# A fused transformer block on one core: the prologue's dense products as couples of 64-row halves

## The chip, the core and the metric

The kernel runs on one core of a Trainium2 chip. A core has a matrix engine (TensorE, PE in the profile; its weight loads are listed apart, as PEld), a vector engine (VectorE, DVE), an engine for activation functions (ScalarE, ACT), a general engine (GpSimd, POOL), and a queue engine (SyncE, SP) that here issues nearly all transfers between the device memory (HBM) and the on-chip memories. TensorE writes into PSUM, which has 128 partitions and eight banks of 512 float32 columns per partition; GpSimd doesn't touch PSUM in this kernel, so a result reaches it by way of a copy of ScalarE.

The metric is the device time of one execution in microseconds.

## The reference

The block takes one sequence of 2048 rows of 512 numbers. Cut to what matters:

```python
mod = (silu(c) @ w_mod).reshape(1, 6, 1, 512)
sa, ca, ga, sb, cb, gb = (mod[:, i] for i in range(6))
h = layernorm(x) * (1 + ca) + sa
q, k, v = split(h @ wqkv)                  # 32 heads of 16
p = softmax(einsum("bhqd,bhkd->bhqk", q, k) * 16 ** -0.5)
x = x + ga * (merge(einsum("bhqk,bhkd->bhqd", p, v)) @ wo)
h = layernorm(x) * (1 + cb) + sb
u = h @ w1 + b1                            # 512 -> 1792
x = x + gb * ((u * tanh(softplus(u))) @ w2)
```

All of it is float32. With 32 heads of only 16 numbers each, the scores of 2048 x 2048 per head are the bulk of the work.

## The kernel before, in words

**Precision.** A dense product is made of three products of rounded operands (type fp32r): high by high, high by low, low by high, where high is the rounded operand and low the rest. `mm3` queues these matmuls; for a contraction of 512 they are 12 of up to 512 columns, 128 rows deep. [...] 

**The attention.** Work goes in steps `t`, 16 of them to an item of four heads and 512 queries (`step`, L1316). Each step has two half steps, numbered `h` (2t and 2t+1), and everything that isn't on the main path is hung onto a half step with `at(h, f)` and issued by `run_hooks(h)`. The engines' instruction streams and the SP queue are in the order of these calls; an instruction that waits holds up all behind it on its engine.

The softmax needs the maximum of each row of scores before the exponentials. So items go through a first pass (`max_tile`, L561, or `max_pair`, L575: scores in the layout queries by keys, and a maximum of VectorE over them) and, 20 steps later (`PRO`), a second one (`score`, L614: scores in the layout keys by queries with the negative maximum as extra rows, and the exponential of ScalarE; `pv`, L628: the product with the values). A maximum of a whole item is turned by `neg_max` and `max_rows` (a transpose through PSUM, a copy on ScalarE, a product on VectorE, four small transfers into the queries' tile, L607).

**The stages.** First (0 to 47 us) comes the layer norm of x, its transposes, and the first slices of the key, query and value products (L325 to L543). Then comes the *prologue*, the steps t = -20 to -1, which this change is about: it has only the first pass, and beside it dense units. Then comes the *main stage* from t = 0, in which both passes and a dense unit run beside each other as 64-row halves, and last the tail (from some 1580 us).

**The prologue's step** (L1321 to L1336). Two calls of `max_pair`: each makes two matmuls with 64 rows (two heads of 16 numbers with extra rows, side by side on the two halves of the array) into a pair of neighbouring banks, and one reduction of VectorE over 128 x 1024. Then the hooks, then `whole_units(h, 7.2)`, which issues dense matmuls, all 128 rows deep, worth 7.2 matmuls of 512 columns. The pairs of banks come from a ring of six banks (`ring`, L151), so three pairs; the dense units use the banks "ms" and "acc" in turn.

**The dense units of the prologue.** `plan` (L1426) lists them: the values' first half for blocks 4 to 15 of 128 rows (12 units of 12 matmuls of 256 columns; two units are as long as one other unit), then the query slice 1 for the first 512 rows, the four units of key slice 1, and the first of key slice 2. Each unit's end is a `fin`. For the values (L285) it is a ScalarE copy into a store buffer, and after each fourth a transfer to HBM. For queries and keys (L250) it is a ScalarE copy `qf`, the rounding `qh` and the rest `ql` on GpSimd, and transfers two half steps later. `qh` and `ql` have two buffers, `qf` has one. The weights of a slice are loaded by `slice_load` (L226), rounded on ScalarE and their rest made on GpSimd by `slice_split` (L233); when that happens is in `planned` (L1431) with the exceptions `LATE_SPLIT` and `LATE_LOAD`.

**What else hangs on the prologue's half steps.** Early preparation of six weight tiles of the second dense layer (`early_prep`, L1483: load, rounding and rest on GpSimd, two stores each), the loads of the head pairs 2 and 3 at -22 and -2 (L1538, `load_pair`), of the values of the first item at -3 (L1528, `load_v`), and the four transfers of the maxima of item 0 at -6.

Of the kernel before, what the change touches and what calls it, by code (L numbers as in the profile page):

```python
# [8 lines left out]
F32 = mybir.dt.float32  # L9
# [9 lines left out]
def adaln_block(ctx: ExitStack, tc: tile.TileContext, x, wqkv, wo, w1, b1, w2, c, w_mod, out):  # L19
    nc = tc.nc  # L20
# [22 lines left out]
    CREDIT = 7.2  # L43
    LATE_SPLIT = {3: -8, 4: 4}
    LATE_LOAD = {3: -15, 4: -4, 5: 9}
# [101 lines left out]
    ring_at = [0]  # L147

    kept = []

    def ring(w=1):  # L151
        if w == 2 and ring_at[0] % 2:
            ring_at[0] += 1
        if kept and ring_at[0] % NRING == NRING - 1:
            ring_at[0] += 1
        b = ring_at[0] % NRING
        ring_at[0] += w
        return ring_t[:, b, :] if w == 1 else ring_t[:, b:b + 2, :]

    def bank(tag="ms"):  # L160
        return ring() if tag == "ring" else ps.tile([P, TB], F32, tag=tag, name="bk", bufs=1)

    def free_banks():
# [3 lines left out]
        for i in nc.cur_bb.bb.instructions:  # L167
# [55 lines left out]
    slices = {}  # L223
    put_away = set()
# [17 lines left out]
    def qk_unit(kind, ct, tb, tag):  # L242
# [7 lines left out]
        def fin(h=None):  # L250
            qh = qp.tile([P, TB], F32R, tag="qh", name="qh", bufs=2)
            ql = qp.tile([P, TB], F32R, tag="ql", name="ql", bufs=2)
# [3 lines left out]
            else:  # L256
                qf = pw.tile([P, TB], F32, tag="raw", name="qf", bufs=1)
# [317 lines left out]
    def max_pair(n, jq, kb):  # L575
# [9 lines left out]
        nc.vector.tensor_reduce(out=mxs[n][:, :, jq, kb:kb + 1], in_=pm, op=ALU.max, axis=AX.X)  # L585

# [722 lines left out]

    def maxima(n, u, s, others):  # L1310
# [5 lines left out]
    def step(t):  # L1316
# [4 lines left out]
        if t < 0:  # L1321
# [104 lines left out]
    plan = [(-PRO, 2, 0, range(4, 16)), (-PRO, 0, 1, (0,)), (-PRO, 1, 1, range(NB)), (-PRO, 1, 2, range(NB)),  # L1426
# [4 lines left out]
    def planned(i, a, tag):  # L1431
# [96 lines left out]
    at(-3, lambda: load_v(0))  # L1528
# [9 lines left out]
    for pp, h in ((2, -22), (3, -2)):  # L1538
        at(h, lambda pp=pp: load_pair(pp))
# [3 lines left out]

    for t in range(-PRO, T + 2):
        step(t)
        prep_step(t)
# [33 lines left out]
```

## Time and profile before

| | us |
|---|---|
| median of three runs | 1688.64 |
| lowest and highest of them | 1687.62, 1691.29 |
| profiled execution, its time | 1688.32 |
| its span | 1686.5 |
| PE busy in the span | 1670.4 (99%) |
| DVE busy | 1432.9 (85%) |
| ACT busy | 1357.4 (80%) |
| POOL busy | 812.5 (48%) |

The profile has one row per group of instructions. A row of the timeline gives the start, the length, the engine, the line of the kernel, the operation, what it writes and reads, the shapes and the number of instructions taken together, and in brackets the idle time of the engine before it with what ended that. A row of the chain of waits gives only start, length, engine and line: it is the path on which the end depends. `SPq` rows are transfers being issued by the SP queue, not their landing. In the rows of windows, the columns are the stretch, its length, then busy time and number of instructions of PE, PEld, DVE, ACT and POOL, then the granted clock of TensorE (1.00 is all of it), the busy share of the DMA engines, and GB/s.

### The profile page before, as it was taken

Reading aid. Unit: us, or ns where it says so; the run is one execution under the profiler, and the core shown is the slowest. Engines: PE = TensorE matmul, PEld = TensorE weight load, DVE = VectorE, ACT = ScalarE, POOL = GpSimd, SP = SyncE. Lnnn points to the kernel's source line nnn. Section 1 sums busy time; section 2 is a strip of 40 time slices with the busy share of each in tenths; the row PEclk is TensorE's granted clock in tenths of the full one; section 3 lists DMA queues with packets and bytes.
Section 4 is the critical chain, followed back from the end, with each engine's and each line's share of the span. In section 5 each row is a group of like instructions: output and inputs, shape, how many; then the busy total and the mean of one; then the engine's idle time right before and its main releaser. Section 6 shows DMA issues by size and latency. Waiting matters only on the chain.

```text
span 1686.5 us, 33920 instructions
## 1 busy us (share of the span) xinstructions
PE 1670.4 (99%) x12491; PEld 924.4 (55%) x12491; DVE 1432.9 (85%) x2372; ACT 1357.4 (80%) x2612; POOL 812.5 (48%) x839
## 2 busy tenths in 40 slices
PE   8999999999999999999999999999999999999998
PEld 6755655555445455555555455555555455555687
DVE  6998888888999988888889888888889888883377
ACT  7257777777778988888878998888878988889674
POOL 5555224655313664556323565556323664555442
PEclk9999999999999999999999999999999999999999
DMA  8877656777755334434355434534344433534261
GB/s 261 264 251 188 157 145 197 205 228 218 225 136 161 97 93 104 120 81 130 82 137 161 106 77 98 139 80 122 100 133 120 130 93 81 149 97 135 76 227 63
DMA packets 114983, 239.00 MB, mean 142 GB/s; under 512 B 24500, under 2 KB 50120, under 8 KB 108864
## 3 DMA queue, kind: packets, MB, share of 16 engines
q1 hardware_dynamic: 114808, 236.82, 49.7%
q8 instruction: 99, 1.62, 0.4%
q14 instruction: 68, 0.56, 0.1%
q10 hardware_dynamic: 8, 0.00, 0.0%
HBM read 180.48 MB, written 51.45 MB: 138 GB/s over the span
## 4 chain that ended last, share of the span: by engine, by line
PE 92%; DVE 3%; ACT 2%; DMA 1%; issue 1%; POOL 0%; SPq 0%; ACTq 0%; DVEq 0%; POOLq 0%
PE bk L636 29%; PE ring L618 22%; PE ring L569 19%; PE bk L134 11%; PE bk L127 3%; PE ring L127 2%; PE ring L1249 2%; DVE mx L571 2%; ACT pr L621 1%; PE ring L583 1%; DMA qa<-mt 0%; PE ring L952 0%; PE ring L598 0%; DMA xt<-in_A_x 0%; PE ring L134 0%
## 5 line engine op out<-in xcount | busy, mean ns | idle before, releaser
L571 DVE TENSOR_REDUCE mx<-ring 128x1 f32<-128x512 f32 x1968 | 1221.9, 681 | 150.9 <-PE ring L569 136.2
L621 ACT ACTIVATE pr<-ring 128x512 f32<-128x512 f32 x2048 | 1078.7, 603 | 207.8 <-PE bk L134 116.3
L569 PE MATMUL ring<-ka,qa 64*128 64x512 f32 x1968 | 818.3, 429 | 1.3 <-ACT pr L621 1.0
L618 PE MATMUL ring<-qa,ka 64*128 64x512 f32 x2048 | 759.0, 402 | 3.2 <-ACT pr L621 2.0
L636 PE MATMUL bk<-pr,vg 128*32 128x512 f32 x4096 | 545.1, 604 | 0.0
L569 PEld LDWEIGHTS ring<-ka,qa 64*128 64x128 f32 x1968 | 350.6, 184 | 326.4 <-DVE mx L571 251.4
L618 PEld LDWEIGHTS ring<-qa,ka 64*128 64x128 f32 x2048 | 373.6, 184 | 192.2 <-DVE mx L571 113.3
L134 PE MATMUL bk<-h,w 64*128 64x512 f32 (+1 forms) x1080 | 277.8, 390 | 0.0
L134 PE MATMUL bk<-w,a_h 64*128 64x512 f32 x632 | 210.8, 413 | 0.0
L134 PEld LDWEIGHTS bk<-h,w 64*128 64x128 f32 x1080 | 178.5, 184 | 9.2 <-ACT pr L621 1.5
L636 PEld LDWEIGHTS bk<-pr,vg 128*32 128x32 f32 x4096 | 81.2, 108 | 135.8 <-issue 126.5
L134 PE MATMUL bk<-w,a_l 64*128 64x512 f32 x316 | 124.0, 392 | 0.0
L134 PEld LDWEIGHTS bk<-w,a_h 64*128 64x128 f32 x632 | 106.7, 184 | 3.4 <-ACT hb L830 0.8
L1008 POOL TENSOR_TENSOR y<-yd,y 128x512 f32<-128x512 f32 x44 | 56.8, 1292 | 88.9 <-ACT yd L1007 79.5
L842 POOL TENSOR_SCALAR qq<-ee 128x512 f32<-128x512 f32 x25 | 15.5, 620 | 169.3 <-ACT ee L836 169.3
L858 POOL TENSOR_TENSOR qq<-qq,rr 128x512 f32<-128x512 f32 x42 | 54.1, 1289 | 85.8 <-ACT rr L852 85.8
L844 POOL TENSOR_TENSOR hb<-hb,ee 128x512 f32<-128x512 f32 x42 | 54.1, 1288 | 79.6 <-DVE ee L840 77.6
L134 PE MATMUL bk<-w,o_hl 64*128 64x512 f32 x288 | 79.3, 405 | 0.0
L96 POOL TENSOR_TENSOR a_l<-hb,a_h 128x512 fp32r<-128x512 f32 x53 | 73.1, 1379 | 4.4
L134 PEld LDWEIGHTS bk<-w,a_l 64*128 64x128 f32 x316 | 58.3, 184 | 2.8
L93 POOL TENSOR_SCALAR qh<-qf 128x512 fp32r<-128x512 f32 x27 | 16.7, 620 | 88.3 <-ACT qf L258 68.1
L134 PE MATMUL bk<-h_h,wl 64*128 64x512 f32 x168 | 57.3, 421 | 0.2 <-ACT pr L621 0.2
(222 smaller groups left out, 1901.3 us busy)
## 6 DMA issues: line engine op xcount, KB each, us to landing
ka<-kscr SPq DMA_DIRECT2D x124, 384.0 KB
w<-w2scr SPq DMA_DIRECT2D x56, 512.0 KB
w<-w1scr SPq DMA_DIRECT2D x46, 512.0 KB
vg<-vscr SPq DMA_DIRECT2D x32, 552.0 KB
qa<-qscr SPq DMA_DIRECT2D x124, 100.0 KB
kscr<-qh SPq DMA_DIRECT2D x16, 512.0 KB
qscr<-qh SPq DMA_DIRECT2D x32, 256.0 KB
w2scr<-hl SPq DMA_DIRECT2D x14, 512.0 KB
```

The costliest lines, as they stand in the source:

```text
L96: (nc.gpsimd if eng == "p" else nc.vector).tensor_sub(lo, src, hi.bitcast(F32))
L127: nc.tensor.matmul(acc, l, r, start=start, stop=stop)
L134: i = nc.tensor.matmul(acc, l[64 * g:64 * g + 64], r[64 * g:64 * g + 64], start=start and not then, stop=bool(stop and then))
L569: nc.tensor.matmul(pm, qt[64 * s:64 * s + 64, qs * P:(qs + 1) * P], kt[64 * s:64 * s + 64, kb * TB:(kb + 1) * TB], start=True, stop=True)
L571: nc.vector.tensor_reduce(out=mxs[n][:, s, 4 * j + qs, kb:kb + 1], in_=pm, op=ALU.max, axis=AX.X)
L618: nc.tensor.matmul(p_, kt[64 * s:64 * s + 64, kc * P:(kc + 1) * P], qt[64 * s:64 * s + 64, :], start=True, stop=True)
L621: e = nc.scalar.activation(pr, p_, AF.Exp, scale=SCALE)
L636: nc.tensor.matmul(accs[n][32 * h:32 * h + 32, :], vgs[n][:, o:o + 32], pts.pop((t, h)), start=(kc == 0), stop=(kc == 15))
L844: (nc.vector if tail else nc.gpsimd).tensor_mul(hb, hb, ee)
L858: nc.gpsimd.tensor_mul(qq, qq, rr)
L1008: nc.gpsimd.tensor_add(y[i], yd, y[i])
L1249: nc.tensor.matmul(po[i // 2][:, i % 2, :], l[:, s], w[:, r, :], start=(f == 0 and j == 0), stop=(f == FT - 1 and j == 2))
```

## The change

**Couples.** The prologue's dense matmuls are no longer issued with 128 rows. A generator (`lanes`) takes twelve slots at a time into one bank (a query or key unit, or two value units in the two halves of a bank); two such banks make a couple. A first turn over the couple issues, slot by slot, rows 0 to 63 of the one and rows 64 to 127 of the other, a second turn the remaining halves. Two couples are interleaved: first turn of one, first turn of the other, second turn of the one, second turn of the other. The second turn waits for a small ScalarE copy `seen`, which the next `max_pair` behind the first turn makes from its own scores. Each call of `max_pair` is followed by a call of `dense_slots` for three or four slots (3, 3, 3, 3, 4, 4, 4, 4, 4, 4 and again), where before two `max_pair` were followed by 7.2 slots at once. A couple's four or so ends (`fin`) come together, one half step after its second turn.

**Banks.** During the prologue the ring of `max_pair` has four banks, two pairs. The other two banks of the ring, "ms" and "acc" are the four beds of the two couples. After the last step the ring is six banks again.

**Order and buffers.** The query unit comes before the values. A slice is split directly in the `fin` that calls for it, where that is before half step -4, and key slice 2 is loaded at half step 7 behind that. Query and key units that end at half steps -4 to 2 take `qh` and `ql` from eight spare tiles (tiles that the attention's output uses later) and `qf` from the buffers of the exponentials.

**Loads.** Pair 3 is loaded at -10 (was -2), the first item's values at -7 (was -3).

**Dependencies.** The pass that declares instructions on different ring banks independent looks back over 96 instructions of the ring (was 32).

```diff
-    CREDIT = 7.2
-    LATE_SPLIT = {3: -8, 4: 4}
-    LATE_LOAD = {3: -15, 4: -4, 5: 9}
+    LATE_SPLIT = {4: 4}
+    LATE_LOAD = {4: -4, 5: 9}
...
-        b = ring_at[0] % NRING
+        b = ring_at[0] % ring_of[0]
...
-                for j, b, others, theirs in seen[-32:]:
+                for j, b, others, theirs in seen[-96:]:
...
+            late = h is not None and -4 <= h < 3
+            if late and not spares:
+                for v in range(2):
+                    both = ap.tile([P, DK, TB], F32R, tag=f"o_{v}", name="late", bufs=1)
+                    spares.extend(both[:, i, :] for i in range(DK))
+            if late:
+                qh, ql = spares.pop(), spares.pop()
...
+                qf = (ap.tile([P, TB], F32, tag=f"p{len(spares) // 2 % 2 * 2}", name="qf", bufs=3) if late else
+                      pw.tile([P, TB], F32, tag="raw", name="qf", bufs=1))
...
+        if waiting:
+            seen = ap.tile([P, 2], F32, tag="seen", name="seen", bufs=2)
+            e = nc.scalar.copy(seen, pm[:, :, 0])
+            for c in waiting:
+                c["after"] = e
+            waiting.clear()
...
+    COUPLES = 6
+    now, waiting = [0], []
+    beds = [ring_t[:, NRING - 2, :], ring_t[:, NRING - 1, :], "ms", "acc"]
+    def lanes():
+        def take():
+            bed = bank(beds[0])
+            beds.append(beds.pop(0))
+            slots, fins = [], []
+            while len(slots) < 12:
+                while not units or now[0] < units[0][0]():
+                    yield None
+                half = len(fins) * TB // 2
+                unit = units.pop(0)[1]
+                fins.append(unit(bed[:, half:]))
+                n = 2 if pe_queue[0][0].shape[-1] <= TB // 2 else 1
+                ms = [(*m[:3], m[3] and half == 0, m[4] and len(slots) * n + len(pe_queue) == 12 * n) for m in pe_queue]
+                slots += [ms[j:j + n] for j in range(0, len(ms), n)]
+                pe_queue.clear()
+            return slots, fins
+        def couple():
+            a = yield from take()
+            b = yield from take()
+            return {"two": (a, b)}
+        def turn(c, p):
+            (a, fa), (b, fb) = c["two"]
+            for j, both in enumerate(zip(a, b)):
+                for k in range(max(len(x) for x in both)):
+                    for x, g in zip(both, (p, 1 - p)):
+                        if k < len(x):
+                            mm_half(x[k], g, c["after"] if p and not j and not k else None, p)
+                yield len(a) - j - 1
+            if not p:
+                waiting.append(c)
+                return
+            for fin in fa + fb:
+                at(now[0] + 1, lambda fin=fin, h=now[0] + 1: fin(h))
+        for _ in range(COUPLES // 2):
+            c1 = yield from couple()
+            yield from turn(c1, 0)
+            c2 = yield from couple()
+            yield from turn(c2, 0)
+            yield from turn(c1, 1)
+            yield from turn(c2, 1)
+    def dense_slots(h, most):
+        now[0] = h
+        for _ in range(most):
+            if not next(lane, 0):
+                return
...
-            if second and tm % 16 == 15:
-                neg_max(tm // 16)
-            run_hooks(2 * t + 1)
+                if i and second and tm % 16 == 15:
+                    neg_max(tm // 16)
+                if not i:
+                    run_hooks(2 * t + 1)
+                dense_slots(2 * t + 1, 3 if (2 * tm + i) % 10 < 4 else 4)
...
-            whole_units(2 * t + 1, CREDIT)
+            if t == -1:
+                for _ in lane:
+                    pass
+                ring_of[0] = NRING
...
-    plan = [(-PRO, 2, 0, range(4, 16)), (-PRO, 0, 1, (0,)), (-PRO, 1, 1, range(NB)), (-PRO, 1, 2, range(NB)),
+    plan = [(-PRO, 0, 1, (0,)), (-PRO, 2, 0, range(4, 16)), (-PRO, 1, 1, range(NB)), (-PRO, 1, 2, range(NB)),
...
-                    at(split_at[i + 2], lambda: slice_split(*plan[i + 2][1:3], hi_eng="p" if h > 0 else "a"))
+                    split = lambda: slice_split(*plan[i + 2][1:3], hi_eng="p" if h > 0 else "a")
+                    split() if h < -4 else at(split_at[i + 2], split)
...
-    at(-3, lambda: load_v(0))
+    at(-7, lambda: load_v(0))
...
-    for pp, h in ((2, -22), (3, -2)):
+    for pp, h in ((2, -22), (3, -10)):
...
+    ring_of[0] = NRING - 2
     for t in range(-PRO, T + 2):
```

More of the change, by code (lines that the diff above doesn't have):

```diff
@@ L147, in adaln_block @@
     ring_at = [0]
+    ring_of = [NRING]
     kept = []
@@ L160, in bank @@
     def bank(tag="ms"):
+        if not isinstance(tag, str):
+            return tag
         return ring() if tag == "ring" else ps.tile([P, TB], F32, tag=tag, name="bk", bufs=1)
@@ L223, in adaln_block @@
     slices = {}
+    spares = []
     put_away = set()
@@ L250, in fin @@
         def fin(h=None):
-            qh = qp.tile([P, TB], F32R, tag="qh", name="qh", bufs=2)
-            ql = qp.tile([P, TB], F32R, tag="ql", name="ql", bufs=2)
+            late = h is not None and -4 <= h < 3
[5 more added lines that the diff above has]
+                qh, ql = spares.pop(), spares.pop()
+            else:
+                qh = qp.tile([P, TB], F32R, tag="qh", name="qh", bufs=2)
+                ql = qp.tile([P, TB], F32R, tag="ql", name="ql", bufs=2)
             if h is None:
@@ L256, in fin @@
             else:
-                qf = pw.tile([P, TB], F32, tag="raw", name="qf", bufs=1)
+                qf = (ap.tile([P, TB], F32, tag=f"p{len(spares) // 2 % 2 * 2}", name="qf", bufs=3) if late else
+                      pw.tile([P, TB], F32, tag="raw", name="qf", bufs=1))
                 nc.scalar.copy(qf, acc)
@@ L1308, in whole_units @@
                 cur["fin"] = None
+    COUPLES = 6
[41 more added lines that the diff above has]
+            yield from turn(c2, 1)
+    lane = lanes()
+    def dense_slots(h, most):
[3 more added lines that the diff above has]
+                return
     def maxima(n, u, s, others):
```

## The prediction

> **What bounds the kernel now.** I read the page's totals first, then windows over the first 130 us, since all that the change reorders runs there, then the chain of waits and the timeline from 45 to 110 us.
>
> ```profile
> PE 1670.4 (99%) x12491; PEld 924.4 (55%) x12491; DVE 1432.9 (85%) x2372; ACT 1357.4 (80%) x2612; POOL 812.5 (48%) x839
> ```
> ```profile
> 65.00:70.00 5.00, 5.00 (x38) 4.00 (x37) 4.53 (x5) 1.07 (x3) 4.83 (x6) 1.00 1.05 348
> 100.00:105.00 5.00, 4.38 (x31) 2.68 (x29) 5.00 (x10) 4.33 (x10) 1.89 (x2) 1.00 1.00 246
> ```
> ```profile
> 63.00 0.66 PE ring L583 x4
> 63.66 1.87 PE bk L127 x14
> ...
> 94.05 0.66 PE ring L583 x4
> 94.72 1.82 PE bk L127 x7
> ...
> 100.58 1.12 ACT pr L621 x2
> ...
> 102.48 0.23 PE bk L134
> ```
>
> PE is busy all the time, in the prologue too, but with DVE close behind (4.53 of 5 us) and the DMA engines full. In the chain a prologue step is 0.66 us for four score matmuls and 1.8 to 1.9 us for the dense ones. The row at 102 us is the main stage's rate: one pair of 64-row matmuls per 0.23 us. Four score matmuls would thus be 0.46, not 0.66.
>
> ```profile
> 65.46 0.74 PE L583 MATMUL ring<-ka,qa 64*128 64x512 f32 x4
> 66.00 2.36 DVE L585 TENSOR_REDUCE mx<-ring 128x2 f32<-128x1024 f32 x2 [0.15 <-PE ring L583]
> 66.12 0.54 PEld L127 LDWEIGHTS bk<-wl,h_h 128*128 128x128 f32 x4 [0.37 <-issue]
> ...
> 95.21 1.09 PE L127 MATMUL bk<-h_h,wh 128*128 128x512 f32 x4
> 96.14 0.40 PE L127 MATMUL bk<-h_h,wl 128*128 128x512 f32 x1
> ```
> ```profile
> L585 DVE TENSOR_REDUCE mx<-ring x40: 1212/1216/1227, 48.8 to 98.2; 128x2 f32<-128x1024 f32 x40
>   PE ring L583: 2.5, 9
> ```
>
> The weight loads pause 0.37 us, with no releaser, where the forms change from 64 to 128 rows; this is the lost time. A full matmul of 512 columns costs (1.09 - 0.40) / 3 = 0.23 us, the same as a pair of halves, so couples save nothing but the two changes of form in each step. Two reductions back to back take 2.36 us, one 1.216, so their pitch is 1.144 us; the 40 starts (48.8 to 98.2) are 1.267 us apart on average where 1.144 would do. DVE could be 0.12 us quicker in each half step.
>
> **The change part by part.**
>
> *Couples.* PE's work in the prologue is 40 score pairs and 144 slots, 184 x 0.235 = 43.2 us. VectorE's forty starts need 39 x 1.144 = 44.6 us and two small things more. So the bound passes from PE to DVE, and the gain is capped by it: if nothing else stood in the way, the last reduction would start at 48.83 + 44.6 + 0.67 = 94.1 instead of 98.2.
>
> *Two pairs of banks in place of three, at the start.* The ring's call count is 21 at the first `max_pair`. By six banks it gets 4 and 5; by four it gets 2 and 3, and bank 2 (20 modulo 6) holds the last key unit of the stage before.
>
> ```profile
> 48.09 0.62 ACT L89 CAST wh<-wr 128x512 fp32r<-128x512 f32 x1
> 48.23 0.69 DVE L96 TENSOR_TENSOR ql<-ring,qh 128x512 fp32r<-128x512 f32 x1 [1.25 <-ACT qh L89]
> 48.79 1.29 POOL L96 TENSOR_TENSOR wl<-wr,wh 128x512 fp32r<-128x512 f32 x1 [2.10 <-ACT wh L89]
> ```
>
> DVE reads that bank until 48.92, then PE's pair can go, and 0.54 us (65.46 to 66.00) later the first reduction: 49.55 in place of 48.83, 0.7 us lost. Behind it the query unit, now first, finds its weights (48.71 and 50.08) in time.
>
> *The maxima of item 0.*
>
> ```profile
> 88.85 0.34 DVE L592 TENSOR_REDUCE mm<-mx 128x16 f32<-128x64 f32 x2
> ...
> 89.26 0.28 PE L598 MATMUL ring<-ident,mm 128*32 128x128 f32 x1
> ...
> 91.38 0.33 DVE L601 SCALAR_TENSOR_TENSOR mt<-mh,lows,ring 32x128 fp32r<-32x128 f32 x1
> ...
> 91.77 2.79 SPq L607 DMA_DIRECT2D qa<-mt  x4
> ```
>
> The two DVE pieces stay, 0.67 us. The transpose takes a single bank of the four and makes the next pair skip one, onto banks that the last reduction still reads: that pair comes 0.54 us after it, less the 0.33 that DVE fills with L601, 0.2 us lost. Its form is another one, a pause of the 0.37 kind, of which I count 0.25. The half steps behind it all have four slots, 5 x 0.235 = 1.175 us on PE against 1.144: 0.03 for five of them. Together 0.6 us; the ends are 0.2 (the pair alone) and 1.0 (two full pauses besides).
>
> *Ends of units in bunches; slices split at once.* The query unit's end puts the rounding of key slice 1 onto ScalarE ahead of the copies that empty its two beds.
>
> ```profile
> 59.24 0.43 SPq L230 DMA_DIRECT2D wr<-in_A_wqkv  x1
> 59.78 1.54 SPq L1488 DMA_DIRECT2D ep<-in_B_w  x3
> ...
> 63.54 0.62 POOL L93 TENSOR_SCALAR ep<-ep 128x512 fp32r<-128x512 f32 x1 [8.22 <-DMA ep<-in_B_w]
> 65.09 0.37 ACT L287 COPY vq<-bk 128x256 f32<-128x256 f32 x1 [1.92 <-PE bk L127]
> ...
> 80.24 1.23 SPq L268 DMA_DIRECT2D qscr<-qh  x2
> 88.44 0.62 POOL L93 TENSOR_SCALAR qh<-qf 128x512 fp32r<-128x512 f32 x1 [3.32 <-DMA qscr<-qh]
> ...
> 95.49 0.59 ACT L258 COPY qf<-bk 128x512 f32<-128x512 f32 x1 [3.87 <-PE bk L127]
> 96.87 1.28 POOL L96 TENSOR_TENSOR ql<-qf,qh 128x512 fp32r<-128x512 f32 x1
> ```
>
> The load is issued at 59.24 whatever the prologue does, as what precedes it on SP is unchanged; a transfer issued 0.5 us later took 3.8 us, so it lands at about 63.0. Then 0.62 + 0.59 + 2 x 0.37 = 1.95 us of ScalarE: beds free at 65.0. The third couple asks for them at half step 14 of the prologue's 40, 49.55 + 13 x 1.144 + 0.3 = 64.7. PE waits 0.3. DVE has 1.144 - 0.54, some half a microsecond, in hand, but four-slot half steps follow that don't win it back: 0.2 us lost. With the longest landing seen (80.24 to 88.44, 8.2 us) it would be 4.7; lower end 0. GpSimd's 1.28 + 0.62 per key unit moves but never gates PE: the four late units, 1.9 us each from about 94 on, are over by 102, and the exponentials' buffers that they borrow are wanted in step 1 (first two) and step 3 (last two). Their spare `qh`/`ql` spare GpSimd the 3.32 us wait; nothing waits for GpSimd there, so 0. Six copies `seen` of two columns: most of a turn of 12 slots lies between copy and use, 0; without that cover a matmul's 0.40 and at most a copy's 0.37 each. The look-back of 96: a read that is 32 ring instructions old is over a step old, and no bank is kept as long; 0.
>
> *Loads.* Pair 3 and the values have their readers beyond t = 2; no wait of before falls on them, gain 0. But `load_v` now stands on SP ahead of L607, and itself waits for the values' last store (below).
>
> *The hand-over.* Sum for the last reduction's start: 49.55 + 44.6 + 0.67 + 0.6 + 0.2 = 95.6. PE issues that pair 0.54 earlier, then 5 x 0.235: main stage from 96.25.
>
> ```profile
> 98.95 0.50 PE L618 MATMUL ring<-qa,ka 64*128 64x512 f32 x1
> ...
> 99.13 0.59 ACT L258 COPY qf<-bk 128x512 f32<-128x512 f32 x1 [3.06 <-PE bk L127]
> 99.29 0.39 PE L134 MATMUL bk<-h_h,wh 64*128 64x512 f32 x1
> ...
> 99.62 0.60 ACT L621 ACTIVATE pr<-ring 128x512 f32<-128x512 f32 x1
> ```
>
> That is 2.7 us ahead of 98.95. In the kernel before, one copy `qf` precedes the exponentials, which start 0.67 us into the stage; now two units end together, the first matmul of the next unit wants one of their banks, and two copies of 0.59 precede: the last slot ends 0.2 us into the stage, so the exponentials start at 0.2 + 1.18 = 1.4, that is 0.7 later. The chain runs through ACT there (row at 100.58), so 0.7 us is given back. Both ends: 0.3 (ScalarE's slack later) and 1.0.
>
> Sum: -2.7 + 0.7 = -2.0 us; bounds -3.4 to -0.8. The later stages keep their instruction order. The profiled execution took 1688.32 us (span 1686.5 and 1.8 around it), 0.3 under the median of 1688.64, so the median goes to 1686.6, 0.12% less. About 0.2%, 3.4 us, is what a measurement of this kernel can tell from no change.
>
> **The rivals.**
>
> *Slower: slots of values with values.* In 48 of the slots both halves are two matmuls of 256 columns, so four weight loads per slot. No row of before has that; the nearest has three.
>
> ```profile
> 159.89 0.18 PEld L134 LDWEIGHTS bk<-wh,h_h 64*128 64x128 f32 x1
> ...
> 160.00 0.30 PEld L134 LDWEIGHTS bk<-wh,h_h 64*128 64x128 f32 x2
> ...
> 160.47 0.40 PE L134 MATMUL bk<-wl,h_h 64*128 64x256 f32 x2
> 160.71 0.40 PE L134 MATMUL bk<-wl,h_h 64*128 64x256 f32 x2
> ```
>
> Loads on one half of the rows start 0.11 us apart. Were four of them serial, a slot would be 0.44 us. The 14 half steps concerned would take 48 x 0.44 + 14 x 0.235 = 24.4 us on PE against 16.0 on DVE: 7.9 more after half a microsecond in hand, 1694.5. The gain is gone from 0.32 per slot, and it is 0.2% slower from 0.39. Against it: two value halves with their loads, and a score's load beside, keep 0.24 per slot, so at least three don't serialise; and DVE leaves room for (16.0 - 3.3) / 48 = 0.26. [...]
>
> *No gain: a transfer is late.* L607 brings the maxima that the first score needs. The values' last store goes out at about 81.4 (half step 28, 49.55 + 27 x 1.144, and a microsecond of copies), `load_v` waits for its landing, L607 behind it. Landing in 3.8 us costs nothing, since L601 itself comes at about 89.5; in 8.2 us it moves L607 to 89.6 + 1.0 (`load_v`'s own issue, row below), 1.1 late, and its 2.8 us of issuing and a landing must fit before 96.3.
>
> ```profile
> 96.16 1.01 SPq L556 DMA_DIRECT2D vg<-vscr  x1
> ```
>
> Each microsecond beyond is paid in full, as is a late slice at 63 us. DMA at 1.05 speaks for it; the first two of the four L607 serving the first step speaks against. Two such microseconds give 1688.6.
>
> *Faster: the cap is reached.* PE runs ahead where it has three slots, and the hand-over hides under ScalarE's slack: the whole 4.1 us, 1684.5. For it: DVE's 39 pitches are the only hard limit. Against: the held first pair and the two copies are in the order of issue.
>
> **How the numbers follow.** Forecast 0.43, no gain 0.20 (a quarter of it beyond 0.2% slower), faster 0.20, slower 0.17. So faster 0.20, same 0.43 + 0.15 = 0.58, slower 0.22. The forecast's own range is 1685.2 to 1687.8; to hold eight in ten it reaches to 1683.5 (the cap, and the lowest run's distance of 1 us) and to 1692.0, a slot of 0.39.
>
> **What would show it.** No L127 in the prologue; L585 starting at 49.5, then every 1.14 us, last at 95.6, with PE waiting for DVE there; the first L618 at 96.3 and the first exponential 1.4 behind it. Wrong, if half steps with values are over 1.2 us, if ScalarE waits for `wr` or the first score for `mt`, or if later stages differ by more than they shift.

## The result, and the profile after

The changed kernel takes 1693.71 us (median of 12 runs, 1691.08 to 1696.12) where the kernel before takes 1688.32 (12 runs, 1685.87 to 1691.29): a ratio of 1.0029, 95% interval 1.002 to 1.0038. It is slower, and lies outside the range of 1683.5 to 1692.0.

The profiled execution of the changed kernel took 1691.93 us, 1.8 under its median; the one of before took 1688.32, its median. So the two profiles show 3.6 us of the 5.4 (spans 1690.1 and 1686.5).

First the totals, from the page of the changed kernel:

```profile
PE 1667.0 (99%) x12707; PEld 932.1 (55%) x12707; DVE 1431.6 (85%) x2372; ACT 1357.3 (80%) x2618; POOL 812.5 (48%) x839
```

Nothing there tells of a loss: PE is 3.4 us less busy than before. The loss is in the prologue's windows (the number behind POOL's is the granted clock):

```profile
60.00:70.00 10.00, 10.00 (x140) 9.47 (x138) 10.00 (x10) 3.01 (x9) 6.33 (x7) 1.00 0.68 203
70.00:80.00 10.00, 9.83 (x129) 9.35 (x126) 10.00 (x10) 1.52 (x6) 6.46 (x8) 1.00 0.85 270
80.00:90.00 10.00, 5.23 (x40) 4.50 (x39) 5.35 (x5) 1.75 (x4) 3.29 (x4) 0.82 1.02 292
90.00:97.00 7.00, 6.52 (x42) 4.79 (x42) 5.25 (x7) 0.43 (x2) 1.55 (x2) 0.77 1.06 309
```

From 60 to 80 us it goes as forecast: DVE is busy for 10.00 of 10 us. The pitch of the reductions is 1.13 to 1.14 us from the third to the thirtieth (1.265 on average before). From 80 on every engine stands, and the granted clock falls. The timeline of ScalarE there, and then of SP:

```profile
80.25 0.37 ACT L299 COPY vq<-bk 128x256 f32<-128x256 f32 x1 [2.32 <-PE bk L133]
87.72 0.62 ACT L88 CAST wh<-wr 128x512 fp32r<-128x512 f32 x1 [7.10 <-DMA wr<-in_A_wqkv]
88.25 0.37 ACT L299 COPY vq<-bk 128x256 f32<-128x256 f32 x1
88.51 0.59 ACT L270 COPY qf<-bk 128x512 f32<-128x512 f32 x1
```
```profile
77.26 0.94 SPq L1578 DMA_DIRECT2D w1scr<-ep  x2
79.00 0.38 SPq L233 DMA_DIRECT2D wr<-in_A_wqkv  x1
79.78 4.80 SPq L1578 DMA_DIRECT2D w1scr<-ep  x4
...
95.08 0.33 SPq L568 DMA_DIRECT2D vg<-vscr  x1
```

The raw weights of key slice 2 (`wr`) are issued at 79.00 and have landed by 87.7. ScalarE is to round them at 80.6, in the middle of the ends of the last values, and waits 7.10 us. Two copies that empty beds of the couples stand behind that. In the kernel before the same transfer went out at nearly the same time, but the rounding was wanted 6 us later, when it was there:

```profile
79.61 0.38 SPq L230 DMA_DIRECT2D wr<-in_A_wqkv  x1
```
```profile
86.59 0.62 ACT L89 CAST wh<-wr 128x512 fp32r<-128x512 f32 x1
```

The view of waits of the changed kernel (engine, line, what it waited for: us in total, times, longest) shows the wait handed on, from the landing to ScalarE, to PE, to DVE:

```profile
ACT wh L88 <- DMA wr<-in_A_wqkv: 9.1, 2, 7.1
...
DVE mx L597 <- PE ring L595: 7.9, 5, 5.9
PEld bk L133 <- ACT vq L299: 5.2, 1, 5.2
```

The 31st pitch of the reductions is 7.115 us instead of 1.131. The last reduction starts at 101.79 (forecast 95.6, before 98.16), the main stage at 103.05, the first exponential at 103.67 (forecast 97.65, before 99.62), the first product with the values at 110.15 (before 106.01). From there to the last instruction it is 1580.0 us, before 1580.5: the later stages are unchanged, and the prologue has all of the loss.

### The profile page after: what moved, and what is told of

Read it like the earlier page. It is cut to its first block, busy times and chain, and to the rows that moved or that the text cites. A ratio compares the mean times of both kernels' runs of the same rounds, so it can differ in the third digit from the quotient of the medians.

```text
span 1690.1 us, 34360 instructions
## 1 busy us (share of the span) xinstructions
PE 1667.0 (99%) x12707; PEld 932.1 (55%) x12707; DVE 1431.6 (85%) x2372; ACT 1357.3 (80%) x2618; POOL 812.5 (48%) x839
## 3 DMA queue, kind: packets, MB, share of 16 engines
q8 instruction: 100, 1.64, 0.4%
## 4 chain that ended last, share of the span: by engine, by line
PE 89%; DVE 4%; DMA 3%; ACT 2%; issue 1%; SPq 0%; POOL 0%; ACTq 0%; DVEq 0%; POOLq 0%
PE bk L654 29%; PE ring L636 22%; PE ring L581 19%; PE bk L133 11%; PE ring L1267 2%; PE ring L126 2%; DVE mx L583 2%; ACT pr L639 1%; PE bk L126 1%; DVE mx L597 1%; PE ring L133 1%; DMA ka<-kscr 1%; DMA kscr<-qh 0%; DMA qa<-mt 0%; PE ring L970 0%
## 5 line engine op out<-in xcount | busy, mean ns | idle before, releaser
L636 PE MATMUL ring<-qa,ka 64*128 64x512 f32 x2048 | 759.1, 402 | 3.4 <-ACT pr L639 1.9
L636 PEld LDWEIGHTS ring<-qa,ka 64*128 64x128 f32 x2048 | 373.8, 184 | 192.3 <-DVE mx L583 113.2
L133 PE MATMUL bk<-h_h,wl 64*128 64x512 f32 x192 | 63.3, 426 | 0.3 <-ACT pr L639 0.3
L133 PE MATMUL bk<-h_h,wh 64*128 64x512 f32 x192 | 53.9, 413 | 5.1 <-ACT vq L299 4.8
```

The lines of the kernel that those rows point to most:

```text
L133: i = nc.tensor.matmul(acc, l[64 * g:64 * g + 64], r[64 * g:64 * g + 64], start=start and not then, stop=bool(stop and then))
L636: nc.tensor.matmul(p_, kt[64 * s:64 * s + 64, kc * P:(kc + 1) * P], qt[64 * s:64 * s + 64, :], start=True, stop=True)
```

## The experiments

In all of them the edit is to the changed kernel if nothing else is said. Times are medians; the kernel before ran beside each (1687.99 to 1689.02). "First" and "last" are the starts of the first and the last of the 40 reductions.

**The late slice earlier.** The theory is that the landing of slice 2 is the loss. Its load is hung six half steps earlier.

```diff
-    LATE_LOAD = {4: -4, 5: 9}
+    LATE_LOAD = {3: -27, 4: -4, 5: 9}
```

> One change to the changed kernel: the raw weights of key slice 2 are loaded at half step -27 instead of -21, so their transfer is issued some 10 us earlier on the SP queue and should have landed before ScalarE asks for them. Theory 1 (the late slice holds up ScalarE, ScalarE holds the two beds, and the stop halves TensorE's clock): ScalarE's wait of 7.1 us for wr goes, the gap of 5.9 us in the reductions goes, the second stretch of half clock goes with its 1.3 us; the main stage starts at 96 to 97 instead of 103.05, and the time falls by 6 to 7.5 us, to about 1686.5. Rival (the transfers as a whole are short of time, or the couples cost something of their own): another transfer is late in its place, the gap moves but stays over 3 us, and the time stays at 1690 to 1694.

Measured: 1694.32 us, ratio 1.0034 (1.0024 to 1.0044). The stall is gone: the slice goes out at 65.93, no pitch before the 32nd is over 1.25 us, and the last reduction starts at 94.79, earlier than the 95.6 of the forecast. But nothing is won, and the rival of the expectation has it (another transfer is late in its place): the first score (L636) now waits for the maxima, whose four transfers (L625) SP could issue only from 92.64 on (timelines of PE and of SP):

```profile
94.54 1.09 PE L133 MATMUL bk<-h_l,wh 64*128 64x512 f32 x8
99.85 0.76 PE L636 MATMUL ring<-qa,ka 64*128 64x512 f32 x1 [4.22 <-DMA qa<-mt]
```
```profile
85.09 0.66 SPq L306 DMA_DIRECT2D vscr<-vq  x1
85.80 1.35 SPq L321 DMA_DIRECT2D qa<-qscr  x2
87.19 1.61 SPq L330 DMA_DIRECT2D ka<-kscr  x2
89.27 0.38 SPq L284 DMA_DIRECT2D kscr<-qh  x1
90.02 0.34 SPq L285 DMA_DIRECT2D kscr<-ql  x1
92.22 0.33 SPq L568 DMA_DIRECT2D vg<-vscr  x1
92.64 3.32 SPq L625 DMA_DIRECT2D qa<-mt  x4
```

The product that they are made from was ready at 88.31. Pair 3 (L321, L330) and the values' rows (L568), both moved ahead by the change, are in front of them on SP. After the pause the granted clock is halved from 98.05 on for 10.24 us.

**The first pair onto free banks**, alone and with the early slice.

```diff
     ring_of[0] = NRING - 2
+    ring_at[0] = 24
```

> One change to the changed kernel: the ring's count is set so that the first pair of scores of the prologue takes banks 0 and 1, not 2 and 3, one of which the stage before still reads. Theory 1: the late slice stays, so the big gap stays; only the start gets better, by the 0.6 us that the first pair waited and, if TensorE's clock stays full, by 1.1 us of slow half steps: -0.5 to -1.8 us against the changed kernel, about 1692.3. Theory 3 (the bad start is the main cost): over 3 us better. If TensorE's clock still halves at 48.9, the query unit's wait for its weights is enough to halve it.

> The early load of key slice 2 and the free first pair together. Theory 1: the two gains add, -7 to -9 us against the changed kernel, 1684.5 to 1686.5, which is 2 to 4 us under the kernel before. Rival (couples or transfers cost something of their own): not under the kernel before.

Measured: 1693.37 us, 1.0027 (1.0016 to 1.0038), and 1694.15, 1.0035 (1.0022 to 1.0047). With the counter alone the first reduction is at 47.83, directly behind VectorE's `ql`, and the dip of the clock at 48.87 is gone. Yet pitches of 3.9 us at the 15th (slice 1) and of 5.4 at the 31st take it back: ScalarE now comes to both slices before they have landed (12.0 us in two waits). With the early slice 2 besides, the wait for the maxima is there again, 4.7 us, and the theory that the two gains add has missed. A microsecond won ahead of a late transfer is a microsecond more of waiting for it.

**ScalarE's order.** Is it the place of the rounding in the middle of a bunch of ends?

```diff
-                    split() if h < -4 else at(split_at[i + 2], split)
+                    split() if h < -20 else at(split_at[i + 2], split)
```

> One change to the changed kernel: key slice 2 is split one half step after the end of the values, as its own hook, and not in the middle of it, so ScalarE empties both beds before it waits for the raw weights. If only the order on ScalarE is at fault, the gap goes and the time falls by 6 us or more. If the late landing itself is at fault, as theory 1 has it, the next couple still can't start without the rounded slice: the gap stays within 1 us of what it was and the time falls by 0 to 1.5 us.

Measured: 1693.3 us, 1.0027 (1.0018 to 1.0036). The copies go first now, and still the 31st pitch is 6.7 us; PE waits for the rounded weights themselves (a row of its view of waits). It is the landing, not the order.

```profile
PEld bk L133 <- ACT wh L88: 5.1, 1, 5.1
```

**The moved loads.** Three kernels: the loads put back with the early slice; the loads put back alone; and the kernel *before* with nothing but the loads moved.

```diff
-    at(-7, lambda: load_v(0))
+    at(-3, lambda: load_v(0))
...
-    for pp, h in ((2, -22), (3, -10)):
+    for pp, h in ((2, -22), (3, -2)):
```

> The early load of key slice 2 as in the first run of this kind, and besides the loads of pair 3 and of the first values back at half steps -2 and -3, where the kernel before has them. In the run with the early load alone the last reduction started at 94.8 us, but the first score waited 4.2 us for the rows of the maxima (mt), which stood on the SP queue behind the values' load until 92.6, and TensorE's clock halved for 10 us at the start of the main stage. Theory 1b (the values' load ahead of the maxima on SP takes what the late slice no longer takes): the maxima's transfers are issued at 90 or before, the main stage starts at 95.5 to 97, no half clock follows, and the time is 1684 to 1687. Rival (transfers as a whole are short of time in a shorter prologue): the maxima land at 98 or later all the same, and the time stays above 1689.

> The changed kernel with the values' rows of the first block (load_v) back at half step -3 and pair 3 back at -2; the raw weights of key slice 2 stay at -21. Theory (two tenants of SP's queue: the raw slice that lands late costs the last reduction about 6 us, and SP held by pair 3 and by load_v ahead of the rows of maxima costs the first score about 4 us, and either of them alone fills the time that the other leaves): the gap before the 31st reduction stays near 6 us, last reduction about 101 to 102, first exponential 102.5 to 103.7 as in the changed kernel, 1692.5 to 1694.0. Rival (the moved loads alone are the loss, since the kernel with both cures is the only one that gained): 1687 to 1688.5 with the gap before the 31st reduction gone. Rival 2 (the gap is chance in DMA landing): no gap above 2.5 us.

> The kernel before with only the loads of pair 3 and the first values moved to -10 and -7. The values' store lands late, the values' load waits for it on SP, and the maxima's transfers wait behind. In the longer prologue there are 3 us more for it: theory 1b expects the maxima's issue to slip by 0 to 3 us and the first score by 0 to 2 us, time 0 to 2 us longer; if the early loads are good in themselves, the time falls by over 0.5 us.

| | slice 2 loaded at half step -21 | slice 2 loaded at half step -27 |
|---|---|---|
| loads as changed | 1693.71, ratio 1.0029 | 1694.32, ratio 1.0034 |
| loads back | 1692.64, ratio 1.0027 (1.0016 to 1.0038) | 1687.16, ratio 0.9989 (0.998 to 0.9998) |

Neither cure alone gains anything that shows; both together are worth 6 to 7 us and give a kernel that is 0.1% faster than the one before, with an interval that ends just below 1. With the loads back alone the 31st pitch is 7.3 us. With both cures SP issues the rows of maxima from 90.71 on, and the first score waits for the last reduction and no longer for them:

```profile
90.71 3.42 SPq L625 DMA_DIRECT2D qa<-mt  x4
```
```profile
97.56 0.50 PE L636 MATMUL ring<-qa,ka 64*128 64x512 f32 x1 [0.43 <-DVE mx L597]
```

The kernel before with nothing but the loads moved takes 1691.15 us, 1.0012 (1.0003 to 1.0021): the last reduction is as far behind the first as it was (49.3 us; it starts at 97.64), but from there to the main stage it takes 2.65 us in place of 0.79, with 1.8 of waiting for the maxima. So the forecast's "gain 0" for the loads hid a loss.

**Which of the two loads.** Slice 2 early, and one load back at a time.

> The changed kernel with the raw weights of key slice 2 at -27 and only the values' rows of the first block (load_v) back at -3; pair 3 stays at -10. With slice 2 early and both moved loads left where the change put them, the first score waited 4.2 us for the rows of maxima; with both moved back it did not. Theory (load_v is what holds SP: it waits for the last values' stores while the rows of maxima stand behind it): no wait for the rows, first exponential within 2.0 us of the last reduction, 1686.5 to 1688.5. Rival (pair 3's four transfers and the stores that wait for landings hold SP): the wait of 3 us or more stays and the median is 1692 to 1695. If both hold SP a part: 1689 to 1692.

> The same with only pair 3 back at -2; load_v stays at -7. Theory (load_v holds SP): the first score still waits 3 us or more for the rows of maxima, 1691.5 to 1695, with a dip of the granted clock after it. Rival (pair 3): no wait, 1686.5 to 1688.5.

With the values' rows back: 1692.36 us, 1.0023 (1.0013 to 1.0033). With pair 3 back: 1688.25, 0.9997 (0.9988 to 1.0006). The first score's wait is the same in both, 2.85 and 2.92 us: with either load moved the rows of maxima are late. With pair 3 in front SP issues them from 92.30 on; with the values' rows in front, which go out only at 95.66, from 96.10. With both back it was 90.71, and the score didn't wait. The order on SP isn't all of it: from the first issue to the end of the wait it is 7.1 us in the first kernel and 3.2 in the second. So each load holds a part, but both expectations missed: they tied the wait to the time, and the second kernel has the wait and not the loss. What sets the two apart is the clock, by the windows of the first and then of the second:

```profile
100.00:102.00 2.00, 2.00 (x13) 1.67 (x9) 2.00 (x4) 1.66 (x3) 1.55 (x2) 0.53 0.89 310
102.00:104.00 2.00, 1.71 (x9) 0.89 (x8) 1.13 (x2) 0.82 (x2) 0.00 (x0) 0.50 0.86 262
```
```profile
100.00:102.00 2.00, 1.76 (x13) 0.85 (x12) 2.00 (x4) 1.82 (x4) 1.32 (x2) 1.00 0.95 260
102.00:104.00 2.00, 2.00 (x14) 1.30 (x14) 2.00 (x5) 1.44 (x3) 0.00 (x0) 1.00 1.03 226
```

A pause of the same length halved the clock in one for 6.83 us and not in the other; from the first score to the first product with the values it is 9.15 and 6.96 us. In the traces the changes of the clock lie whole steps of 3.41 us apart, on a grid that lies elsewhere in each (last section). The pause falls into one step in the first kernel (0.70 us of matmuls in it) and is shared by two in the second:

```profile
96.70:100.11 3.41, 0.70 (x6) 0.70 (x8) 0.39 (x2) 1.21 (x3) 3.33 (x4) 1.00 0.85 269
```
```profile
94.62:98.03 3.41, 1.72 (x16) 1.07 (x12) 2.09 (x2) 1.07 (x2) 3.33 (x4) 1.00 0.51 162
98.03:101.44 3.41, 2.19 (x15) 1.47 (x15) 1.65 (x3) 1.68 (x4) 3.21 (x4) 1.00 0.52 168
```

So the dip is a matter of chance, and whether every execution of the first kernel has it the one profile can't tell. Of the 4.0 us between the two traces 2.2 lie between the first score and the first product with the values, and 1.7 behind it; that the dip makes all of the 4.1 us between the medians is not shown.

**More on top of both cures.** First the banks again (the ring's counter at 24).

> The kernel with both cures (raw weights of key slice 2 at -27, load_v at -3, pair 3 at -2) and the ring's counter set to 24 ahead of the prologue, so that the first pair of keys finds both its banks free. Its profile without the counter had three slow pitches at the start (1.291, 1.706, 1.353 us against 1.131, together 0.96 us) and one dip of the granted clock at 49.01. Theory (every microsecond of the prologue's reductions reaches the end): first reduction 47.8 to 48.0 instead of 48.65, no dip near 49, last reduction 0.8 to 1.8 us earlier than 96.29, 1685.4 to 1686.6. Rival (the earlier start only uncovers the next late slice or POOL, as in the kernel that also moved key slice 1): gaps of over 2 us after the 14th reduction, 1687 to 1688.5.

Measured: 1687.38 us, 0.9998 (0.9989 to 1.0007). The first reduction is at 48.5, the slow first pitches are gone, and the 15th has grown from 2.17 to 3.92 us: the rival. Slice 1 is late in turn. It stands on SP behind the last rows of keys, at 61.15. Three kernels issue it earlier: ahead of those rows (together with both cures, without and with the counter), and one step of the first stage earlier still, behind the rows of keys of the step before (with the counter). The edit of the first two:

```diff
+            if tb == 3:
+                slice_load(1, 1)
             for pp in range(2):
                 load_k(pp, tb)
...
-    at(-2 * PRO, lambda: slice_load(*plan[2][1:3]))
```

> As the run before in this call, and besides the ring's count set so that the first pair finds free banks, and the raw weights of key slice 1 loaded before the last key block's loads, some 6 us earlier. Theory: none of ScalarE's waits for wr is left, reductions start at 48 and run every 1.13 us, last at 93 to 94; the main stage starts at 94 to 96 and the time is 1683 to 1686, below the kernel before by 0.15 to 0.3%. Rival: the first score still waits for the maxima's rows until 98 or later, and the time is within 1.5 us of the kernel before or above it.

> The kernel with both cures, and the raw weights of key slice 1 issued ahead of the last rows of keys of pairs 0 and 1 instead of behind them. With both cures SP stood at those rows until 61.1 and ScalarE then waited 4.4 us for slice 1; the pitch after the 15th reduction was 2.17 us. Theory (SP's order is the whole of that gap): no pitch above 1.5 us between the 10th and the 30th reduction, last reduction 1.0 us earlier (95.2), 1685.8 to 1687.0. Rival (the earlier landing only brings POOL's half of the slice to the front, which waits for the expert weights, as in the kernel that issued slice 1 earlier still): gaps of over 2 us at the 18th to the 32nd reduction, 1687.5 to 1689.

> The same with the ring's counter at 24 ahead of the prologue. Theory (each stall of the reductions that goes is time won at the end): first reduction near 47.9 to 48.5, last one 94.2 to 95.0, 1684.5 to 1686.5. Rival (the first pair's microsecond is given back at the next late slice or at POOL, as it was with the counter alone): last reduction within 0.5 us of the kernel without the counter, or later, 1686.5 to 1688.5.

The earliest place gave 1688.15 us, 0.9993 (0.9984 to 1.0002), with new pitches of 2.6 and 4.1 us, around which PE waits for the rest of a slice (`wl`, 3.1 us in two waits) that GpSimd makes behind the early weight tiles. The place ahead of the last rows gave **1685.8 us, 0.9987 (0.9978 to 0.9996)**, with the counter 1686.06, 0.9986 (0.9977 to 0.9995); both beat the kernel before, by 0.1%, and which of the two is better isn't told apart. The theory of the first holds: no pitch from the 10th to the 30th is over 1.5 us. Windows of it (slice 1 ahead, no counter), and a row of its waits:

```profile
60.00:70.00 10.00, 10.00 (x141) 9.47 (x139) 10.00 (x10) 2.85 (x8) 5.32 (x6) 1.00 0.72 224
70.00:80.00 10.00, 9.83 (x124) 9.39 (x122) 10.00 (x10) 2.39 (x9) 7.26 (x8) 1.00 0.81 246
80.00:90.00 10.00, 8.42 (x68) 6.63 (x66) 9.06 (x11) 1.21 (x5) 5.01 (x5) 1.00 1.02 322
90.00:97.00 7.00, 6.57 (x58) 5.15 (x56) 6.38 (x7) 2.27 (x6) 3.69 (x4) 1.00 1.01 335
```
```profile
DVE mx L599 <- PE ring L597: 1.6, 3, 0.7
```

The work from 80 to 97 us is done at full clock; DVE waits 1.6 us for PE in the whole prologue, never more than 0.7 at once (L599 is the reduction, two lines lower than in the changed kernel). The last reduction starts at 95.05, and at 93.95 with the counter; the first exponential at 96.93 and 95.84.

**The late units' own tiles, and the look-back.** Both on top of both cures; the expectation of the second kernel says that it has no tiles, but it is the kernel with the tiles and only the look-back at 32.

```diff
-            late = h is not None and -4 <= h < 3
+            late = False
```

> The kernel with both cures, without the late units' own tiles: qh, ql and qf of the units that end at half steps -4 to 2 use the tiles of all others again. Theory (the tiles pay only where ScalarE would otherwise wait for POOL, which in the profile with tiles has one wait of 2.4 us and one of POOL of 7.5 us): ScalarE's qf copies near 82 and 94 wait 2 to 7 us for POOL, first exponential up to 2 us later, 1687.2 to 1689.5. Rival (the tiles do nothing for the time): 1686.7 to 1687.6 and the first exponential within 0.5 us of 98.17. Rival 2 (the tiles cost: their last readers hold the buffers that the main stage needs): 1685.5 to 1686.7.

> The kernel with both cures, with the list of matmul records that are declared independent back at 32 from 96, without the tiles of the late units' own (the two edits of the change that touch no order of instructions in the prologue's dense work). Theory (32 records are about four slots of couples; a reduction that shares no bank with the matmuls 33 to 96 records back would wait for them without need, but they have ended by then): within 0.5 us of the kernel without the tiles. Rival (false waits between PE and DVE or ScalarE): pitch of the reductions above 1.2 us in the median, 1690 or more.

Without the tiles: 1703.73 us, 1.0092 (1.0078 to 1.0105), some 17 more than with them, and more than either theory had. With the look-back at 32: 1686.42, 0.9994 (0.9985 to 1.0003); it does nothing that shows, and the median pitch isn't slowed. The timelines of GpSimd and of ScalarE without the tiles:

```profile
112.00 0.62 POOL L92 TENSOR_SCALAR qh<-qf 128x512 fp32r<-128x512 f32 x1 [11.07 <-DMA kscr<-qh]
```
```profile
113.99 0.59 ACT L270 COPY qf<-bk 128x512 f32<-128x512 f32 x1 [12.44 <-POOL ql L95]
114.47 1.58 ACT L639 ACTIVATE pr<-ring 128x512 f32<-128x512 f32 x3
```

Four key units end together. With two buffers, GpSimd's third rounding must wait until the store that reads the first has gone out, 11.07 us; ScalarE stands with `qf` behind it, and the exponentials behind that.

**Fewer early tiles.** As the kernel with slice 1 earliest, but with three weight tiles of the second dense layer prepared in the prologue in place of six, so that GpSimd and the DMA engines have less to do there.

```diff
-    EARLY = 6
+    EARLY = 3
```

> As the second of this call, and besides three early weight tiles prepared in the prologue, not six (0.75 MB less read and 1.5 MB less written between 60 and 88 us; the other three are prepared later, among the rest). If the transfers' total is what makes every landing late, the maxima's rows and the slices land sooner: main stage from 94 to 95 and a time below the second run's by 0.5 to 2 us. If only the order on the SP queue matters: within 0.7 us of the second run.

Measured: 1705.05 us, 1.0093 (1.0079 to 1.0107). The prologue is quicker (first product with the values at 104.5 against 108.15 with six tiles), but from there on it takes 1599.8 us instead of 1579.0, which neither theory had. The tiles are of `w1`, the product 512 -> 1792. The other preparations follow one after the other in the main stage, and the kernel starts the products with prepared weights only behind the last of them. With three more its store goes out at 471.91 us in place of 447.93, and the first such product runs at 492.88 in place of 469.44, the first with `w1` at 553.22 in place of 535.40. At the end these products aren't done: from 1580 to 1600 us PE is busy for 11.68 us (20.00 with six tiles) and DVE for 0.69 (9.29), and PE stands for 6.68 us until GpSimd has rounded an operand of theirs (`a_h`). So the preparation that the prologue carries is wanted in the main stage.

## Why the prediction was wrong

- *Couples, and the bound that passes to DVE*: right. The pitch was forecast at 1.144 and is 1.131; the 128-row products are gone from the prologue; and with the stalls cured the last reduction starts at 96.29 (both cures) and 95.05 (slice 1 earlier too), forecast 95.6.
- *The slower rival, values with values*: refuted. Eight matmuls of 256 columns, two slots, are 0.46 us apart in the changed kernel, 0.23 a slot as elsewhere, not 0.44.

```profile
54.08 0.70 PE L133 MATMUL bk<-wh,h_h 64*128 64x256 f32 x8
54.54 0.71 PE L133 MATMUL bk<-wl,h_h 64*128 64x256 f32 x8
```

- *First pair held by bank 2, 0.7 us*: right in size (its own figures, 48.92 and 0.54, make 49.46 and not 49.55). From the start of VectorE's `ql` to the first reduction it is 1.36 us (47.70 to 49.06), 0.60 before. Not foreseen: after PE's pause of 1.44 us there the clock is halved from 48.87 for 3.41 us. The first two pitches are 1.708 and 1.693, 1.1 us more. This is chance: of the ten traces that have that pause, six have the dip.
- *Maxima of item 0, 0.67 + 0.6*: right, but so exact by luck. The two pitches they lengthen (the 32nd and the 34th) add 1.27 us in the changed kernel, where the first of them runs at half clock, and 1.06 to 2.14 in the cured ones without a dip there.
- *"Slices split at once", 0.2 us*: **this step failed.** Its working took the landing of key slice 1 at 63 us, and in the profiled execution that one cost indeed nothing. Slice 2 went unexamined: the change wants it rounded 6 us earlier, while its load, hung six half steps earlier, goes out at nearly the same time (79.00, before 79.61). SP has other transfers in front of it and issues them from 69.33 to 78.20 with no pause of more than 0.1 us. The slice lands after 8.7 us, with the DMA engines busy for 0.99 of that time, and the 31st pitch loses 5.98 us. The lengths are those that the step itself had as its other end (4.7 us with the longest landing), but there they belong to slice 1. The bounds of the sum, -3.4 to -0.8, leave this end out: the ends given with the single terms add up to -3.0 and +3.2, and with 4.7 in place of 0.2 the sum would be +2.5 us, 1691.1. Slice 1 isn't free either. Nine of the traces have the changed kernel's order up to it; in three, the changed kernel's among them, SP issues it by 59.5 and no pitch suffers, in the other six at 60.2 to 62.5, ScalarE waits 4.4 to 5.2 us for it, and the 15th pitch is 1.0 to 1.9 us longer. A row of the kernel with both cures:

```profile
64.52 0.62 ACT L88 CAST wh<-wr 128x512 fp32r<-128x512 f32 x1 [4.43 <-DMA wr<-in_A_wqkv]
```

- *"Loads: gain 0"*: **failed too, but doesn't show in the result.** The first score was named as a place to look, and the rival "a transfer is late" has the mechanism (`load_v` on SP ahead of the maxima); its price was put at 1 to 2 us, and pair 3 was left out of it. The runs show 2.9 us with either load and 4.2 with both, as soon as the late slice no longer hides it.
- *The hand-over, 0.7*: not there; its total is near by luck. From the last reduction to the first exponential it is 1.88 us, before 1.46; forecast 2.05. But from the main stage's start to the first exponential, where the 0.7 was to come, it is 0.61 (before 0.67, forecast 1.4), and from the last reduction to the main stage's start 1.27 (before 0.79, forecast 0.65).
- *The tiles of their own, 0* ("nothing waits for GpSimd there"): wrong in its reason. Without them it is some 17 us slower: ScalarE waits for GpSimd, and the exponentials for ScalarE.
- *The look-back, 0*: right, with nothing that shows.

The sum, in the profiles: forecast of the last reduction 95.6; first pair 0.5 earlier than forecast (the run itself was 0.5 ahead), the dip 1.1, the late slices 6.0 in place of 0.2, 0.5 less by the quicker pitch, and 0.2 in small ones: 101.7, measured 101.79. The forecast of 1686.6 lies among the kernels that have both cures and lack nothing else (1685.8 to 1688.15) rather than at the one that was changed. Why the median lies 1.8 us above the profiled execution stays open; the 1.0 to 1.9 us that slice 1 costs in six of nine traces would do it, but no other execution of the changed kernel has a trace.

## What to carry to other kernels

When a change lets a consumer run earlier, list every transfer that it waits for, and look where the issuing queue will stand at that time: a load hung onto an earlier step isn't issued earlier if the queue in front of it is held (here six half steps earlier in the program, and issued at 79.00 us against 79.61). Stalls in series hide one another: a cure that gives nothing alone may be worth all of it with the next one (here 0 and 1 us alone, 6 to 7 together), so the next wait is to be read from the trace and cured before the first cure is dismissed. And a bunch of ends needs a buffer for each of its members where a store sets them free (without them GpSimd waited 11.07 us here for one store, and the kernel took some 17 us more).

## What was not expected of the hardware

The granted clock fell after a pause of PE much shorter than the time it stayed down: 1.44 us, and 3.41 us. Windows of the start of the prologue in the changed kernel, and then in the kernel with both cures and slice 1 ahead:

```profile
46.00:50.00 4.00, 2.40 (x15) 1.93 (x16) 2.08 (x3) 1.10 (x2) 1.90 (x3) 0.86 0.94 331
```
```profile
46.00:50.00 4.00, 2.40 (x20) 1.91 (x21) 2.08 (x3) 1.10 (x2) 1.90 (x3) 1.00 0.88 312
```

PE is equally busy, and stands for 1.44 us at one place in the first and 1.45 in the second; one kernel is at half clock for 3.41 us afterwards, the other isn't. In all traces the dips of the prologue last 3.41 us or a multiple (6.83, 10.24, 17.07). Moreover, within each of the 18 traces all changes of the clock lie whole steps of 3.413 us apart (in the changed kernel those at 48.87, 52.28, 86.42 and 93.24 are 0, 1, 11 and 13 steps behind the first), and where this grid lies differs from trace to trace. The dip goes with how busy PE is in one step of the grid. In the six traces in which the pause of 1.44 us is followed by a dip, the matmuls of the step cover 1.80 or 1.81 us; in the four without a dip, 1.97 or more. Here is the step ahead of the dip in the changed kernel, and then the one that holds the pause in the other:

```profile
45.46:48.87 3.41, 1.80 (x9) 0.96 (x9) 1.64 (x3) 1.10 (x2) 1.31 (x2) 1.00 0.82 284
```
```profile
47.02:50.43 3.41, 1.97 (x22) 1.97 (x24) 2.04 (x3) 1.10 (x2) 2.15 (x2) 1.00 1.02 365
```

Of all steps at full clock from 25 to 1575 us in the 18 traces, each of the nine with at most 1.52 us of matmuls is followed by half clock, of the 13 with 1.64 to 1.85 nine are, and none with 1.90 or more. From half clock it took more to come back: behind a step with 3.41 us of matmuls the clock was always full again, behind steps of 2.42 to 3.12 us in one case of six. The ends of matmuls are modelled and some records can be missing, so the limits are rough. So the same stall of 1.44 us cost 1.1 us more in the first two pitches of the changed kernel, where it was followed by a dip, while in four other traces no dip followed it.

One kind of transfer, a raw slice of weights, took 3.6 us from its issue to the end of the wait for it (below, 59.07 to 62.63) and 8.7 us (79.00 to 87.72) in the same execution of the changed kernel; the busy share of the DMA engines was 0.82 in the first stretch and 0.99 in the second.

```profile
59.07 0.43 SPq L233 DMA_DIRECT2D wr<-in_A_wqkv  x1
```
```profile
62.63 0.62 ACT L88 CAST wh<-wr 128x512 fp32r<-128x512 f32 x1 [1.97 <-DMA wr<-in_A_wqkv]
```
